# One more product in two levels, second PSUM banks begun from copies, and three vector jobs moved to ScalarE, in an attention-then-FFN kernel

## The chip, the cores and the metric

The kernel runs on one core of a Trainium2 chip. The metric is the device time of one execution in microseconds (us). Before the change it is 670.1 us, the median of three runs (669.46, 670.10, 670.87). All data are 32-bit floats in the kernel.

## The reference

```python
# batch 4, heads 8, seq 768, head_dim 64; block 64; d_ff 2048
def _attn_ref(q, k, v, lam):
    for b in range(nb):
        intra = einsum('bhic,bhjc->bhij', qb, kb) * Dmask      # lam^(i-j) for i >= j
        intra = einsum('bhij,bhjd->bhid', intra, vb)
        inter = einsum('bhid,bhde->bhie', qb * lam_pow, kv_state)
        out[:, :, sl] = intra + inter
        kb_dec = kb * rev_pow                                   # lam^(block-1-pos)
        kv_state = lam_block * kv_state + einsum('bhsd,bhse->bhde', kb_dec, vb)

def _moe_ref(x, w_in, w_out):          # x: 3072 tokens x 512
    h = x @ w_in                       # 512 x 2048, "the first product"
    g = h - np.tanh(h)
    return g @ w_out                   # 2048 x 512, "the second product"
```

The output of the attention, as 3072 rows of 512, is `x`.

## The kernel before, in words

**Tiling.** The sequence is cut into six groups g = 0 to 5 of 128 positions (of all 4 batch rows: 512 tokens). For a group the attention makes `xt` (512 features by 512 tokens), the first product with tanh makes the hidden values `g11`, `g12`, `g21`, `g22` (a two by two block matrix, each 128 partitions x 4 slices u x 512), and the second product makes four output quarters. Attention runs two groups ahead of the second product.

**Seven products in place of eight.** From group 1 on both big products use the Strassen-Winograd scheme: P1 to P7 with sums of operand blocks (`S1` to `S4` of the weights, `T1` to `T4` of the tokens), and outputs C11 = P1+P2, C12, C21 and C22 from running sums. P1+P6 is needed in three of the four outputs. Some of the seven are made by the same scheme once more ("two levels", `TWICE` for the second product, `INNER` for the first): seven steps of 128x128 blocks in place of four quarters of 128x256.

**First product of group g+1** (g+1 from 2 on; `inner_steps`, L556 to L581, and `seeded`, L485 to L520). P1, P5, P2 and P4 are in two levels. One call of `inner_steps` takes seven steps; a step is four matmuls (one per slice u), so eight records of 128x128 in the trace. The steps fill three PSUM banks (`BANKS`: y, w, z); ScalarE copies a finished corner to SBUF (L573, L575), VectorE adds the others (L577, L580). Then `seeded` handles slice by slice what is left in one level: a bank y is begun from a copy of P1 (L501), P6 is accumulated on it by four matmuls of 128x256 (L509, weights S2 in `ws[u][:, 1]`), z = y + P5 is begun by VectorE (L513); P7 goes to y, P3 to z; tanh on ScalarE and a subtraction on VectorE finish each quarter (L492, L493).

**The loop** (L949 to L1047). For g >= 2 the body is: (a) the slices u = 0 to 3: `seeded` with P7, P3 and P6 mixed with a quarter each of the second product's P1 (`down(g, 1)`); (b) `down(g, 2)`; (c) attention of group g+1 for batch rows 0 and 1 (`att_out`, `att_state`: the state update needs k times a decay, L350, and the state times a factor, L368); (d) the second product's P4, P5, P6, P7 in two levels (`down_twice`), with the scores and the attention of batch rows 2 and 3 between; (e) **the tail**: P3 of the second product turn about with P1 of the first product of group g+1 (`in_turn`), then P5 and P2, then P4 mixed with P6 and one P3 of the slices. In the tail early pieces of the attention of group g+2 (transposes, scores) are run too. g = 1 has its own body (all in one level) and makes the two-level weights: `inner_weights` (four small VectorE sums per slice, then a DMA to `fine_in` in DRAM), `factors_twice` (the same for the second product).

**Orders and queues.** Matmuls run in the written order of the program. A scheduler places VectorE's and ScalarE's instructions among each other; each engine then takes its own list in order. Weight pieces come back from DRAM over POOL's queue through a ring of eight tiles (`piece`). Inputs of the attention come over SP's queue, in written order (`load`, L146): for group g >= 3 seven sets of 16 small transposing loads of q and k (`load_blocks`, L143), then k and v in natural order for batch rows 0 and 1 (`load_natural`, L131), one more set of 16, then k and v for rows 2 and 3. `k_nat` has three buffers for four batch rows, so row 3 waits for row 0's state matmuls.

**Names.** k(g,b) below is the natural-order k of group g, batch row b (tile `k_nat`); `att_decay` multiplies it in place. A step (n,x) is step x of product Pn.

Of the kernel before, what the change touches and what calls it, by code (L numbers as in the profile page):

```python
# [15 lines left out]
AF = mybir.ActivationFunctionType  # L16
# [8 lines left out]
def kernel(  # L25
# [162 lines left out]

    INNER = (1, 5, 2, 4)
    fine_in = dram.tile([len(INNER), 3, 128, NU, 128], F32, name="fine_in")  # L190
# [156 lines left out]

    def att_decay(g, b):
        kp = raw[g, b]["k"].rearrange("s (p j) d -> s p j d", j=2)
        tied(g != 1, nc.vector.tensor_tensor(kp, kp, bwd, op=AL.mult))  # L350

    def att_state(g, bs):
        if g == NG - 1:
            return

        kv = bank("kv", "att", 4).rearrange("d (b p e) -> d b p e", b=2, p=NP)
        for n, b in enumerate(bs):
            kd, vn = raw[g, b]["k"], raw[g, b]["v"]
            if g > 0:
                att_decay(g, b)  # L360
            for p in range(NP):
                for j in range(2):
                    tied(g == 0, nc.tensor.matmul(out=kv[ts(j, 64), n, p, :], lhsT=kd[:, 2 * p + j, :],
                                                  rhs=vn[:, 2 * p + j, :], start=n == 0 and p == 0, stop=True,
                                                  skip_group_check=True))
        st = state[:, bs[0]:bs[0] + 2]
        if g > 0:
            nc.vector.tensor_tensor(st, st, lam_blk, op=AL.mult)  # L368
            nc.vector.tensor_tensor(st, st, kv, op=AL.add)
        else:  # L370
            tied(True, nc.scalar.activation(st, kv, AF.Copy))
# [109 lines left out]
    toks = {}  # L481
    LAND = {1: 12, 5: 22, 2: 11, 4: 21}
    BANKS = {1: ("yb", "z", "att"), 5: ("ya", "att", "z"), 2: ("yb", "w", "att"), 4: ("att", "att", "att")}

    def seeded(g, u, n):  # L485

        def dst(c):
            return hidden(g, c)[:, u]

        def finish(c, src):  # L490
            th = work.tile([128, 2, HB], F32, name="th", tag="th")
            nc.scalar.activation(th, src, AF.Tanh)  # L492
            nc.vector.tensor_tensor(dst(c), src, th, op=AL.subtract)  # L493

        if n == 11:
            nc.vector.tensor_tensor(dst(11), dst(11), dst(12), op=AL.add)
            finish(11, dst(11))
            return
        if n == 6:
            banks[g, u, "y"] = bank("y", "yb" if u % 2 else "ya", 1).rearrange("q (m c) -> q m c", m=2)  # L500
            nc.scalar.activation(banks[g, u, "y"], dst(12), AF.Copy)  # L501
        y = banks[g, u, "y"]
        t = banks[g, u, "z"] if n == 3 else y
        a, bname = FACT[n]
        wt = {"S3": w1[u][:, 0:2, 1], "S2": ws[u][:, 1], "S4": ws[u][:, 2]}[a]
        x = xt[g][bname]
        for m in range(2):
            for kt in range(2):
                nc.tensor.matmul(out=t[:, m, :], lhsT=wt[:, kt, ts(m, 128)], rhs=x[:, kt, :], start=False,  # L509
                                 stop=kt == 1, skip_group_check=True)  # L510
        if n == 6:
            z = banks[g, u, "z"] = bank("zs", "w" if u % 2 else "z", 1).rearrange("q (m c) -> q m c", m=2)
            nc.vector.tensor_tensor(z, y, dst(22), op=AL.add)  # L513
        elif n == 3:
            finish(12, t)
        else:
            for c in (22, 21) if u + 1 < NU else (21, 22):
                nc.vector.tensor_tensor(dst(c), dst(c), y, op=AL.add)  # L518
            for c in (22, 21) if u + 1 < NU else (21, 22):
                finish(c, dst(c))  # L520
# [6 lines left out]
    def a_quarter(n, u, i, k):  # L527
        wt = {1: w1[u][:, 0:2, 0], 2: w1[u][:, 2:4, 0], 4: w1[u][:, 2:4, 1], 5: ws[u][:, 0]}[n]
        return wt[:, k, ts(i, 128)]

    def inner_weights(u, ns):
        for n in ns:
            a11, a12, a21, a22 = (a_quarter(n, u, i, k) for i in range(2) for k in range(2))
            if n in (1, 5):
                t = hidden(GI, 22)[:, u].rearrange("p m (x c) -> p (m x) c", x=2)
            else:
                t = late["pool"].tile([128, 4, 128], F32, name="ws2", tag="sums", bufs=4)
# [15 lines left out]

    STEPS = (1, 2, 6, 5, 7, 3, 4)

    def inner_steps(g, n):  # L556

        y, w, z = (bank(x, tag, 4 if tag == "att" else 1) for x, tag in zip(("y3", "w3", "z3"), BANKS[n]))
        r5 = otile("r5")
        out4 = hidden(g, LAND[n])  # L560
        c11, c12, c21, c22 = (out4[:, :, i, ts(j, 128)] for i in range(2) for j in range(2))
        for x in STEPS:
            b = toks[g, n][x]
            wb = piece(g, ("in", n), x) if x in (3, 5, 6) else None
            dst = w if x == 2 else z if x in (3, 5) else y
            for u in range(NU):
                a = wb.rearrange("p m c -> p (m c)")[:, ts(u, 128)] if wb is not None else a_quarter(
                    n, u, *{1: (0, 0), 2: (0, 1), 7: (1, 0), 4: (1, 1)}[x])
                nc.tensor.matmul(out=dst[:, ts(u, 128)], lhsT=a, rhs=b, start=x in (1, 2, 5) and u == 0, stop=True,  # L569
                                 skip_group_check=True)  # L570
            d = dst.rearrange("q (u c) -> q u c", u=NU)
            if x in (1, 4, 6):
                nc.scalar.activation({1: c11, 4: c21, 6: c12}[x], d, AF.Copy)  # L573
            elif x == 5:
                nc.scalar.activation(r5, dst, AF.Copy)  # L575
            elif x == 7:
                nc.vector.tensor_tensor(c22, r5.rearrange("q (u c) -> q u c", u=NU), d, op=AL.add)  # L577
            else:
                c = c11 if x == 2 else c12
                nc.vector.tensor_tensor(c, c, d, op=AL.add)  # L580
            yield  # L581

# [6 lines left out]
    def in_turn(g):  # L591

        if twice(g, 3):
            turn = [a for x in STEPS for a in (("down", x), (1, x))]
        else:
            turn = [("down", 0), (1, 1), (1, 2), ("down", 1), (1, 6), (1, 5), ("down", 2), (1, 7), (1, 3), ("down", 3),
                    (1, 4)]
        return turn + [(n, x) for x in STEPS for n in (5, 2)]

    def pieces_of(g):  # L600
        if g >= GI:
            yield from ((g, ("in", 4), x) for x in (6, 5, 3))
        for n in (1, 2, 4, 5, 6, 7):
# [79 lines left out]
    def down(g, n):  # L683

        if n in (1, 2) and g >= GI:
            t, first = (bank("plain", "att", 4) if n == 1 else bank("plain", "z", 1)).rearrange(
                "q (m c) -> q m c", m=2), True
        elif n in (1, 2):
# [30 lines left out]
        else:  # L719
            o11 = late["pool"].tile([128, 512], F32, name="o11", tag="o11", bufs=1)  # L720
            nc.vector.tensor_tensor(o11, res[g, 1], t, op=AL.add)
            store(g, 11, o11)
# [226 lines left out]
    for g in range(1, NG):  # L949
        last = g == NG - 1  # L950
        (p0, p1), step = ahead, 0
        for u in range(NU):
# [16 lines left out]
            if u == 0:  # L969
                first = down(g, 1)  # L970
            for n in (1, 7) if u == 0 else (6, 3, 1, 7) if u + 1 < NU else (7, 3, 1):
                if n == 1:
                    next(first)
                else:
                    seeded(g, u + (n == 6), n)
                if n == (7 if u + 1 < NU else 3):
                    seeded_sums(g, u)
        if twice(g, 4):
# [5 lines left out]
        every(down_twice(g, 4, zw[0]) if twice(g, 4) else down(g, 4))  # L984
        run(p1[0:1])
        if g < GI:
            for u in (0, 1):
# [14 lines left out]
        run(p1[2:])  # L1002
        if g < GI:
            for u in (0, 1):
                inner_weights(u, (5,))
# [4 lines left out]
        if g < GI:  # L1010
            for u in (2, 3):
                inner_weights(u, (5,))
            every(factors_twice(2))
            load_quarters(3)
        ahead = attention(g + 2) if g + 2 < NG else ([], [])
# [4 lines left out]
        for i, (kind, x) in enumerate(in_turn(g)):  # L1020
            if kind == 2 and x == 1:
                inner_tokens(g + 1, (2,))
                if g < GI:
                    every(factors_twice(3))
                    load_quarters(4)
            if kind not in parts:
                parts[kind] = inner_steps(g + 1, kind)
            next(parts[kind])
            if (kind, x) in ((1, 7), (2, 2), (2, 7)):
                run(early_pieces[:1])  # L1030
                early_pieces = early_pieces[1:]
        for p in parts.values():
            every(p)
        inner_tokens(g + 1, (4,))
        if g < GI:
            every(factors_twice(4))
        p4 = inner_steps(g + 1, 4)
        for n in (None, None, 6, None, None, 16, None, None, 3, None):
            if n is None:
                next(p4)  # L1040
            else:
                if n == 3:
                    run(early_pieces)
                seeded(g + 1, n // 10, n % 10)
                seeded(g + 1, (6, 16, 3).index(n), 11)
        seeded(g + 1, 3, 11)
        every(p4)  # L1047

# [29 lines left out]
```

## Time and profile before

| what | value |
|---|---|
| median of the runs | 670.1 us |
| the profiled execution | 665.92 us; its span, first to last instruction, 664.2 us |
| granted TensorE clock | 1.000 |
| busy: TensorE matmuls, weight loads, VectorE, ScalarE, POOL | 98, 90, 74, 33, 35 % |
| TensorE's idle time in all | 10.0 us of waits; the longest single one 3.3 us |
| L569 (steps of the first product) | 896 matmul records of 128x128 |
| L509 (slices in one level) | 384 matmul records of 128x256 |
| L350 (decay of k) | 20 x 684 ns on VectorE |
| L368 (state's scaling) | 8 x 678 ns on VectorE |
| DMA on SP's queue | 133,536 packets, 31.5 MB, 24 % of the 16 engines |

Each trace row names line, engine, operation, tiles, shapes and count; a logical fp32 matmul has two records. "Idle before" and the arrow name what the engine waited for. TensorE's records overlap (each begins before the last has drained), so the time of a block of work is read from the starts of successive rows, not from the durations.

### The profile page before, as it was taken

What the parts mean: (1) busy time and instruction counts of PE and PEld (TensorE: products, weight loads), DVE (VectorE), ACT (ScalarE), POOL (GpSimd) and SP (SyncE); (2) the same over time, 40 slices, a digit from 0 to 9 for tenths busy, and PEclk for the clock granted to TensorE, in tenths of its full rate; (3) what the DMA queues carried; (4) which work ended last, traced back from release to release, by engine and by line L of the source; (5) the groups of instructions that cost most, each with busy time, mean ns of one, the idle gap of its engine ahead of it and who ended that gap; (6) DMA issues with size and microseconds to landing.
All of it is one profiled execution on the core that took longest, in us unless ns stands there. A gap on an engine that the chain in (4) does not pass through costs nothing.

```text
span 664.2 us, 13689 instructions
## 1 busy us (share of the span) xinstructions
PE 650.9 (98%) x5112; PEld 597.3 (90%) x5112; DVE 490.4 (74%) x923; ACT 218.7 (33%) x418; POOL 229.2 (35%) x397
## 2 busy tenths in 40 slices
PE   8899999999999999899999999999999999999998
PEld 7788888888888999798999998899998899998897
DVE  4577896745787887588997577988577988457953
ACT  3796835503221112343112243212333212333210
POOL 0001435735432557520345310255320244420261
PEclk9999999999999999999999999999999999999999
DMA  9989888969765999984698773498874376741394
GB/s 212 228 221 258 267 304 233 338 166 252 194 160 136 246 270 298 277 260 94 193 282 251 211 163 93 120 278 241 233 176 98 85 246 205 228 127 48 88 301 153
DMA packets 165475, 136.74 MB, mean 206 GB/s; under 512 B 134688, under 2 KB 135840, under 8 KB 165408
## 3 DMA queue, kind: packets, MB, share of 16 engines
q0 software_dynamic: 31728, 104.36, 49.0%
q1 hardware_dynamic: 133536, 31.50, 24.0%
q8 instruction: 41, 0.67, 0.4%
q14 instruction: 26, 0.21, 0.1%
q10 hardware_dynamic: 144, 0.00, 0.0%
HBM read 109.84 MB, written 25.95 MB: 204 GB/s over the span
## 4 chain that ended last, share of the span: by engine, by line
PE 73%; DMA 14%; SPq 7%; DVE 2%; ACT 2%; issue 1%; POOL 1%; POOLq 0%; ACTq 0%; DVEq 0%
PE y L750 10%; PE y L509 8%; PE plain L697 8%; PE zw L750 8%; PE y L569 7%; SPq L143 5%; PE h L805 5%; DMA q_blk<-in_q_dram 5%; PE zs L509 4%; PE z L569 3%; DMA k_blk<-in_k_dram 3%; PE sp L341 3%; PE op L395 3%; DMA raw<-in_moe_w_in_dram 2%; PE acc L834 2%; PE w L569 2%
## 5 line engine op out<-in xcount | busy, mean ns | idle before, releaser
L659 POOL DMA_DIRECT2D wb<-fine x147 | 79.2, 539 | 187.4 <-PE plain L697 118.0
L697 PE MATMUL plain<-wb,g 128*128 128x256 f32 x352 | 81.2, 380 | 0.0
L697 PEld LDWEIGHTS plain<-wb,g 128*128 128x128 f32 x352 | 66.1, 190 | 8.8
L753 ACT ACTIVATE q<-y 128x128 f32<-128x128 f32 x84 | 23.3, 278 | 128.9 <-PE y L750 128.1
L805 PE MATMUL h<-xt,w 128*128 128x256 f32 x256 | 57.9, 382 | 2.9 <-DVE w L285 2.9
L805 PEld LDWEIGHTS h<-xt,w 128*128 128x128 f32 x256 | 47.7, 190 | 10.5 <-DVE w L285 2.9
L750 PE MATMUL y<-wb,g 128*128 128x128 f32 x384 | 51.1, 278 | 0.0
L573 ACT ACTIVATE g<-y 128x512 f32<-128x512 f32 x48 | 28.5, 594 | 63.8 <-PE y L569 63.8
L492 ACT ACTIVATE th<-g 128x512 f32<-128x512 f32 x48 | 29.5, 628 | 59.1 <-DVE g L518 57.2
L750 PEld LDWEIGHTS y<-wb,g 128*128 128x128 f32 x384 | 46.4, 192 | 1.1 <-issue 0.3
L662 POOL DMA_DIRECT2D wb<-factors x56 | 30.3, 541 | 48.0 <-PE z L569 21.4
L206 POOL DMA_DIRECT2D raw<-in_moe_w_out_dram x16 | 8.7, 546 | 84.7 <-ACT r L282 58.1
L656 POOL DMA_DIRECT2D wb<-fine_in x48 | 25.9, 542 | 33.2 <-PE y L569 13.5
L345 DVE TENSOR_TENSOR ss<-sp,mask 128x512 f32<-128x512 f32 x48 | 30.6, 683 | 7.7 <-PE sp L341 7.7
L750 PE MATMUL zw<-wb,g 128*128 128x128 f32 x256 | 33.8, 275 | 0.0
L493 DVE TENSOR_TENSOR g<-g,th 128x512 f32<-128x512 f32 x48 | 31.7, 686 | 2.8 <-ACT th L492 2.8
L834 PE MATMUL acc<-wt,g 128*128 128x256 f32 x144 | 32.7, 380 | 0.0
L518 DVE TENSOR_TENSOR g<-g,y 128x512 f32<-128x512 f32 x32 | 20.9, 683 | 14.1 <-PE y L509 14.1
L750 PEld LDWEIGHTS zw<-wb,g 128*128 128x128 f32 x256 | 31.2, 192 | 0.0
L834 PEld LDWEIGHTS acc<-wt,g 128*128 128x128 f32 x144 | 27.3, 190 | 3.7
L509 PE MATMUL zs<-xt,ws 128*128 128x256 f32 x128 | 30.6, 381 | 0.0
L509 PE MATMUL y<-tt,ws 128*128 128x256 f32 x128 | 30.3, 379 | 0.0
(219 smaller groups left out, 1484.7 us busy)
## 6 DMA issues: line engine op xcount, KB each, us to landing
wb<-fine POOLq DMA_DIRECT2D x147, 256.0 KB, 3.9
wb<-factors POOLq DMA_DIRECT2D x56, 256.0 KB, 4.4
wb<-fine_in POOLq DMA_DIRECT2D x48, 256.0 KB, 4.5
raw<-in_moe_w_out_dram POOLq DMA_DIRECT2D x16, 512.0 KB, 5.4
v_nat<-in_v_dram SPq DMA_DIRECT2D x24, 256.0 KB, 5.5
k_nat<-in_k_dram SPq DMA_DIRECT2D x20, 256.0 KB, 4.9
fine<-wt POOLq DMA_DIRECT2D x17, 256.0 KB, 4.5
raw<-in_moe_w_in_dram SPq DMA_DIRECT2D x8, 512.0 KB, 6.0
```

The lines of the kernel that those rows point to most:

```text
L143: nc.sync.dma_start(out=x[ts(c, 32), p], in_=blk.rearrange("(r t) a -> t r a", t=32)))
L345: tied(g == 0, nc.vector.tensor_tensor(ss[:, j], sp[j], mask[:, j], op=AL.mult))
L492: nc.scalar.activation(th, src, AF.Tanh)
L493: nc.vector.tensor_tensor(dst(c), src, th, op=AL.subtract)
L509: nc.tensor.matmul(out=t[:, m, :], lhsT=wt[:, kt, ts(m, 128)], rhs=x[:, kt, :], start=False, stop=kt == 1, skip_group_check=True)
L569: nc.tensor.matmul(out=dst[:, ts(u, 128)], lhsT=a, rhs=b, start=x in (1, 2, 5) and u == 0, stop=True, skip_group_check=True)
L659: nc.gpsimd.dma_start(out=t.rearrange("p m c -> p (m c)"), in_=fine[TWICE.index(n_), SUB.index(x_)].rearrange("p u c -> p (u c)"))
L662: nc.gpsimd.dma_start(out=t, in_=factors[XAT[FACT[n_][1]]][:, 2 * x_:2 * x_ + 2, :])
L697: nc.tensor.matmul(out=t[:, m, :], lhsT=a[:, u, kt, ts(m, 128)], rhs=wb[:, kt, :], start=first and u == 0 and m == 0 and kt == 0, stop=u = ...
L750: nc.tensor.matmul(out=dst, lhsT=a[:, u, :], rhs=wb[:, ts(u, 128)], start=x in (1, 2) and u == 0, stop=u == NU - 1, skip_group_check=True)
L805: tied(u == 0, nc.tensor.matmul(out=hm[c][:, m, :], lhsT=w1[u][:, i, a, ts(m, 128)], rhs=xt[0, t][:, i, :], start=m == 0 and i == 0, stop= ...
L834: nc.tensor.matmul(out=acc[n][:, r, :], lhsT=a[:, ts(r, 128)], rhs=b, start=kt == 0 and r == 0, stop=kt == KH - 1, skip_group_check=True)
```

## The change

- **P6 of the first product in two levels.** It gets an entry in `INNER`, its own weights (`inner_weights(u, (6,))`, in the tail of g = 1, staged in the tile of `g21`), token sums and fine pieces, and steps in the tail, turn about with P4. Its results are added to P1 in the tile `g12` itself. The matmuls of `seeded` with n = 6 go; y is begun by a copy of the sum and z by one VectorE addition of two SBUF tiles.
- **Second banks begun from copies.** In `inner_steps` for n other than 1, ScalarE copies step 1's bank into the bank w, and step 2 accumulates there, so that C11 comes out of w in one instruction. For P2 and P6 VectorE's drains add `g12` (P1) at once, so that P1+P2 needs no addition later (the addition at L496 goes).
- **Steps in another order** (`INSTEPS`: 1, 5, 2, 6, 7, 3, 4), other banks, and the slices' order is P7, quarter of `down(g, 1)`, P3.
- **To ScalarE**: the decay of k for groups over 2 (eight activations of 128x64 per batch row with a scale taken from `mask`), the state's scaling for groups over 2 (four of 128x128 per half), and C11 of the second product: P2's bank is begun from a copy of P1's, and C11 is a copy.
- **Moved in g = 1**: `factors_twice(2)` to `(4)` with their loads.

```diff
-    INNER = (1, 5, 2, 4)
+    INNER = (1, 5, 2, 4, 6)
...
     def att_decay(g, b):
+        if g > GI:
+            for h in range(H):
+                k_h = raw[g, b]["k"][:, h, :]
+                nc.scalar.activation(k_h, k_h, AF.Copy, scale=mask[:, h % 2, h // 2, BLK - 1:BLK])
+            return
         kp = raw[g, b]["k"].rearrange("s (p j) d -> s p j d", j=2)
...
-            if g > 0:
+            if 0 < g <= GI:
                 att_decay(g, b)
...
-            nc.vector.tensor_tensor(st, st, lam_blk, op=AL.mult)
+            if g > GI:
+                for p in range(NP):
+                    nc.scalar.activation(st[:, :, p], st[:, :, p], AF.Copy, scale=fwd[:, p, BLK - 1:BLK])
+            else:
+                nc.vector.tensor_tensor(st, st, lam_blk, op=AL.mult)
...
-    LAND = {1: 12, 5: 22, 2: 11, 4: 21}
-    BANKS = {1: ("yb", "z", "att"), 5: ("ya", "att", "z"), 2: ("yb", "w", "att"), 4: ("att", "att", "att")}
+    LAND = {1: 12, 5: 22, 2: 11, 4: 21, 6: 12}
+    BANKS = {1: ("yb", "z", "att"), 5: ("ya", "z", "w"), 2: ("att", "yb", "att"), 4: ("att", "w", "att"),
+             6: ("att", "yb", "att")}
...
         if n == 11:
-            nc.vector.tensor_tensor(dst(11), dst(11), dst(12), op=AL.add)
             finish(11, dst(11))
             return
         if n == 6:
-            banks[g, u, "y"] = bank("y", "yb" if u % 2 else "ya", 1).rearrange("q (m c) -> q m c", m=2)
-            nc.scalar.activation(banks[g, u, "y"], dst(12), AF.Copy)
...
+            nc.scalar.activation(y, dst(12), AF.Copy)
+            nc.vector.tensor_tensor(z, dst(12), dst(22), op=AL.add)
+            return
...
+    INSTEPS = (1, 5, 2, 6, 7, 3, 4)
...
+        more = n in (2, 6)
+        filled = n != 1
+
+        def take(dst, add, src):
+            if more:
+                nc.vector.tensor_tensor(dst, add, src, op=AL.add)
+            else:
+                nc.scalar.activation(dst, src, AF.Copy)
...
+            if x == 1:
+                nc.scalar.activation(w if filled else c11, y if filled else d, AF.Copy)
+            elif x == 2:
+                if filled:
+                    take(c11, s11, d)
+                else:
+                    nc.vector.tensor_tensor(c11, c11, d, op=AL.add)
+            elif x == 6:
+                take(c12, s12, d)
             elif x == 5:
-                nc.scalar.activation(r5, dst, AF.Copy)
+                take(r, s22, d)
...
+        return turn + [(n, x) for x in INSTEPS for n in (5, 2)] + [
+            (4, 1), (4, 5), (4, 2), (6, 1), (4, 6), (6, 5), (4, 7), (6, 2), (4, 3), (6, 6), (4, 4), (6, 7), (6, 3),
+            (6, 4)]
...
-                "q (m c) -> q m c", m=2), True
+                "q (m c) -> q m c", m=2), n == 1
+            if n == 1:
+                low[g] = t
+            else:
+                nc.scalar.activation(t, low.pop(g), AF.Copy)
...
-            nc.vector.tensor_tensor(o11, res[g, 1], t, op=AL.add)
+            if g >= GI:
+                nc.scalar.activation(o11, t, AF.Copy)
+            else:
+                nc.vector.tensor_tensor(o11, res[g, 1], t, op=AL.add)
...
-            for n in (1, 7) if u == 0 else (6, 3, 1, 7) if u + 1 < NU else (7, 3, 1):
+            for n in (7, 1, 3) if u == 0 else (7, 3, 1) if u + 1 < NU else (7, 3):
...
+            if u == 1 and GI <= g < NG - 2:
+                for b in (0, 1):
+                    att_decay(g + 1, b)
...
         run(p1[0:1])
+        if GI <= g < NG - 2:
+            for b in (2, 3):
+                att_decay(g + 1, b)
...
+            if (kind, x) in ((4, 2), (4, 6), (4, 7), (4, 3)):
+                seeded(g + 1, (2, 6, 7, 3).index(x), 11)
```

The scheduler's placement in the changed program: the eight activations for k(g+1,0) and those for k(g+1,1), written at u = 1 of the slices of group g, stand on ScalarE already in the tail before, among the drains of P4: after step (4,1)'s copy and two tanh comes the first of k(g+1,0); behind it, in this order, two more tanh, the drains of (4,5), (4,2), the copy of (6,1) and the drain of (4,6), mixed with the rest of k(g+1,0); then k(g+1,1), the last drain of P4, the two copies into y, and k(g+1,2). k(g+1,3) stands between the copies of the second product's P4. SP's list of transfers is the same as before.

## The prediction

> **What bounds the kernel now.** First I read the page's busy times, then who waited for whom.
>
> ```profile
> PE 650.9 (98%) x5112; PEld 597.3 (90%) x5112; DVE 490.4 (74%) x923; ACT 218.7 (33%) x418; POOL 229.2 (35%) x397
> PE y L569 <- DVE g L577: 3.3, 1, 3.3
> ```
>
> TensorE is the bound: it idles 10 us in all, and only one wait after the first 100 us is long, 3.3 us. So matmuls taken away count in full, and so does each us in which TensorE stands. What a block costs is read from starts in TensorE's timeline (tail of g = 2):
>
> ```profile
> 382.36 1.95 PE L569 MATMUL y<-tt,w 128*128 128x128 f32 x16
> 384.15 1.06 PE L569 MATMUL w<-tt,w 128*128 128x128 f32 x8
> 385.04 1.89 PE L509 MATMUL y<-tt,ws 128*128 128x256 f32 x8
> 386.77 1.05 PE L569 MATMUL y<-tt,wb 128*128 128x128 f32 x8
> ```
>
> A step of eight 128x128 records takes 0.89 us, eight records of 128x256 take 1.73. The first row holds step (2,4) and then (4,1), which so starts at 383.25. Next, how that one wait came about (VectorE's timeline, then TensorE's):
>
> ```profile
> 271.62 0.69 DVE L577 TENSOR_TENSOR g<-r,y 128x512 f32<-128x512 f32 x1 [3.15 <-PE y L569]
> 277.05 0.69 DVE L645 TENSOR_TENSOR gS<-gS 128x512 f32<-128x512 f32 x1 [4.75 <-DMA gS<-factors]
> 277.66 0.68 DVE L577 TENSOR_TENSOR g<-r,y 128x512 f32<-128x512 f32 x1
> ...
> 278.40 2.05 PE L569 MATMUL y<-tt,w 128*128 128x128 f32 x16 [3.31 <-DVE g L577]
> ```
>
> L577's bank was full long before, but L645 stood ahead of it on VectorE and waited 4.75 us for a transfer; so L577 was late, and TensorE after it. An engine's list is not left out of order here: a wait for a transfer stops what stands behind it. [...]
>
> Last, the queue that brings k (SP's timeline):
>
> ```profile
> 278.65 14.58 SPq L143 DMA_DIRECT2D q_blk<-in_q_dram  x16
> 293.34 0.42 SPq L131 DMA_DIRECT2D k_nat<-in_k_dram  x1
> 293.81 0.58 SPq L131 DMA_DIRECT2D v_nat<-in_v_dram  x1
> 294.50 0.80 SPq L131 DMA_DIRECT2D k_nat<-in_k_dram  x1
> ...
> 381.01 8.48 SPq L143 DMA_DIRECT2D q_blk<-in_q_dram  x16
> 389.58 0.38 SPq L131 DMA_DIRECT2D k_nat<-in_k_dram  x1
> ...
> 390.70 2.51 SPq L131 DMA_DIRECT2D k_nat<-in_k_dram  x1
> ```
>
> k(3,0) is issued at 293.34 (3.4 us to landing: there at 296.7) and k(4,0) at 389.58 (5.0: 394.6), because seven sets of 16 small loads stand before them. VectorE asked for k(3,0) only at 320.65 (L350), so this lateness was free.
>
> **Part by part.**
>
> *P6 in two levels.* Taken away per group: four slices of eight 128x256 records, 4 x 1.73 = 6.91 us. Added: seven steps, 7 x 0.89 = 6.25. Saved 0.66 for each of four groups: -2.6 us.
>
> *Drains.* Per group the inner steps go from 12 to 19 large VectorE additions (3, 2, 2, 6, 6 for P1, P5, P4, P2, P6); L496's four and C11's one go; four small token sums come. That is 2 large ones at 0.60 us (spacing of L681's rows) and 4 of 0.29 more, 2.4 us, and 3.6 less in groups 3 and 4, where decay and scaling leave. The tail of g = 2 has room: VectorE is busy 9.6 of 16 us from 368 to 384 and 8.3 of 12 from 384 to 396. In the slices TensorE has 3 x 1.73 = 5.18 us per slice now (P6 is gone from 6.91), VectorE nine operations, 5.43. The lag, 4 x 0.25, is covered by `down(g, 2)` (6.9 us) and the attention (3.9), since sums are needed only by the next product. Priced at nothing; without cover 1 us per group. The copies into second banks (0.6 us each on ScalarE) have two or more steps, 1.8 us, before their bank is used, and P1's copy for C11 the 3.5 us of the last slice.
>
> *Weights in g = 1.* 16 sums of 0.28 us, four writes of 192 KB, three more pieces of 256 KB per group. They lie ahead of the first wait below, which swallows up to 16 us of lateness.
>
> *State's scaling.* Eight activations of 128x128 (278 ns, L753's row) per group after `att_out`'s reads; they end before the second copy of `down_twice` is due. Nothing.
>
> *Decay on ScalarE, first place: the tail of g = 1.* The eight activations of k(3,0) stand among P4's drains. No row has a 128x64 activation. From 594 ns at 512 and 278 at 128 elements it is 225 ns; bounds 140 (two copies in a row overlap by 90, L399) and 278. [...]
>
> Without the old 3.3 us wait, (2,4) starts at 275.1 and (4,1) at 276.0. TensorE then does (4,1), the scores (1.1 us), (4,5), (4,2), (6,1), (4,6), (6,5), and at 282.5 needs the drain of (4,6), which must be out of y before (4,7). On ScalarE that drain stands behind k(3,0). When does k(3,0) land? As before at 296.7; but once TensorE stops, POOL's ring of eight stops too, so the last set of 16, which took 14.6 us beside POOL's transfers, goes faster (the fastest set in SP's timeline takes 7.6: landing 290), while the new weight traffic delays it (300, if 1.6 MB at some 290 GB/s are half in its way). At 282.5 four of the 16 are out at the old pace; twelve at 7.6 / 16 take 5.7, and 0.4 and 3.4 more give 292. With 2 us for the new traffic I take 294. From landing to the end of that drain ScalarE has six activations of k and six of 128x512 (0.6 each): 1.35 + 3.6 = 4.95 us. So TensorE goes on at 298.95, having stood 16.4 us. Then eight steps (7.1) and sixteen blocks of 1.73 (seven, three and both quarters of `down`: 27.6) lead to `att_out` at 333.7; before, it began at 321.56 (L389). **+12.2 us**, the lost 3.3 us wait and this group's 0.66 in it; bounds +8 and +18.
>
> What is late next: k(3,1), 3.1 us behind, finds ScalarE 5 us behind; k(3,2), 12.2 behind, is asked for 14 behind. Both covered, by 1.8 us at the least.
>
> *Second place: the tail of g = 2.* SP starts group 4's sets after k(3,3), issued at 325.07 when row 0's state matmuls are done; I count from there. k(4,0) lands at +69.5. TensorE reaches (4,1) at 383.25 - 325.07 = +58.2, and (4,7) after 1.1 + 6 x 0.89 at +64.7. It goes on at 69.5 + 4.95 = +74.5 (9.7 us), and gets to `att_out` at +109.2 against 425.43 - 325.07 = 100.4. **+8.8 us.** The pace is steady: group 4's seven sets took 62.9 us, group 5's 64.1; with landings from 3.1 to 7.3 us the bounds are +6 and +12.
>
> *k(3,3) and k(4,3)* are asked for after the second copy of `down_twice`'s P4, 3.1 us into it. k(4,3) landed at 432.0, 2.7 us in; the next copy is due at 5.4 us, and seven activations end at 4.7. Nothing.
>
> *Tails of g = 3 and 4* have no decay (the condition on g): -0.66 each, -1.3.
>
> **Sum.** 12.2 + 8.8 - 1.3 = +19.7 us. On the profiled execution, 665.9 (span 664.2), that is 685.6; the median of the runs is 4.2 above that execution, so 670.1 + 19.7 = **689.8 us**.
>
> **Rivals.**
>
> *No wait binds* (ScalarE gets k in time, the change does what it is for): 670.1 - 2.6 - 3.3 = 664.2. For it: ScalarE is busy 33% only. Against: k(3,0) would have to land 16 us earlier, with SP issuing without a gap from 215 to 293. Chance 0.04.
>
> *Only the first binds*, if group 4's sets run at the fastest pace, 7 x 7.6 = 53 us, and k(4,0) lands 9.6 us earlier: the second place gives -0.9 in place of 8.8, so 680.1. For it: POOL's traffic shifts; against: 62.9 and 64.1 in two groups. Chance 0.12.
>
> *VectorE becomes the bound of the slices*: the uncovered lag of 1 us in each of four groups on top of the forecast, 694. For it: 5.43 against 5.18; against: the cover above. Chance 0.10.
>
> *The first wait is longer*: the new weight writes hold SP's set back further than 300, or k(3,2) takes more than 1.8 us longer and ScalarE waits a second time, before the first tanh of the slices: +6 or more, about 697. For it: the DMA engines are 92 to 97% busy from 236 to 292. Chance 0.16.
>
> *Forecast*: both places as worked out. Chance 0.58, its own range 683 to 697.
>
> **How the numbers follow.** The low end is the second rival's, 680; the high end takes both upper bounds, 670.1 + 18 + 12 - 1.3 = 699. Left out is the first rival and the far end of the last, under 2 in 10. A measurement of this kernel tells 0.2%, 1.3 us, from no change; faster by more only with the first rival, 0.04; within it only if both waits nearly vanish, 0.01; slower 0.95.
>
> **What would show it.** In the tails of g = 1 and g = 2 of the changed kernel: ScalarE idle before a 128x64 activation of `k_nat`, released by its DMA, some 14 and 8 us long; right after it TensorE idle at a step of the first product, released by ScalarE's drain, near 16 and 10 us; none in the tails of g = 3 and 4. L509 with 256 records in place of 384. Wrong would be: those waits absent, a VectorE release in the slices, or a wait at k(3,2), k(3,3).

## The result, and the profile after

The changed kernel takes 702.4 us (median of six runs, 699.6 to 705.9); the kernel before, run beside it, 669.7. The ratio is 1.0495, 95% interval 1.0453 to 1.0537. The forecast was 689.8 with a range up to 699: the sign and the two waits were right, the size was 12.6 us short. A time is the median of all runs, but a ratio leaves out an execution over 1.5% above the fastest of its kernel, and there are two: 687.3 us with the decay back on VectorE, and 712.7 with the quarters back and the decay on ScalarE.

First the two waits, in the view of who waited for whom (us in total, count, longest):

```profile
ACT k_nat L352 <- DMA k_nat<-in_k_dram: 26.7, 4, 14.8
...
PE y L589 <- ACT g L580: 21.6, 2, 10.8
...
PE z L589 <- DMA wb<-fine_in: 4.9, 4, 2.0
```

ScalarE waits for k in four places, of which two are long (14.81 and 10.35 us), and TensorE twice behind these, as forecast. The last line was not forecast: TensorE also waits for weight pieces of the first product. Now the first place, ScalarE's timeline:

```profile
301.36 0.59 ACT L352 ACTIVATE k_nat<-k_nat,mask 128x64 f32<-128x64 f32 x2 [14.81 <-DMA k_nat<-in_k_dram]
301.86 0.61 ACT L502 ACTIVATE th<-g 128x512 f32<-128x512 f32 x1
...
305.32 0.58 ACT L580 ACTIVATE g<-y 128x512 f32<-128x512 f32 x1
305.80 2.48 ACT L352 ACTIVATE k_nat<-k_nat,mask 128x64 f32<-128x64 f32 x10
```

and TensorE's in the same microseconds:

```profile
291.71 1.16 PE L589 MATMUL y<-tt,wb 128*128 128x128 f32 x8 [2.42 <-DMA wb<-fine_in]
293.51 1.71 PE L589 MATMUL z<-tt,wb 128*128 128x128 f32 x8 [0.64 <-DMA wb<-fine_in]
305.95 2.07 PE L589 MATMUL y<-tt,w 128*128 128x128 f32 x8 [10.74 <-ACT g L580]
307.82 1.91 PE L589 MATMUL w<-tt,ws 128*128 128x128 f32 x8
309.52 1.74 PE L589 MATMUL z<-tt,wb 128*128 128x128 f32 x8
311.10 1.06 PE L589 MATMUL y<-tt,wb 128*128 128x128 f32 x8
```

The drain of (4,6) at 305.32 stands behind k(3,0), and releases step (4,7) at 305.95. The first three steps behind the stand then take 311.10 - 305.95 = 5.15 us in place of 3 x 0.89 = 2.68. The windows (length; busy time of TensorE's matmuls, its weight loads, VectorE, ScalarE, POOL; granted clock; share of the DMA engines; GB/s) tell why:

```profile
294.00:305.90 11.90, 1.21 (x6) 0.92 (x5) 2.26 (x4) 4.54 (x13) 2.59 (x5) 0.50 0.99 273
305.90:311.10 5.20, 5.15 (x25) 5.15 (x25) 2.30 (x4) 2.38 (x10) 0.54 (x1) 0.51 0.66 146
311.10:318.00 6.90, 6.90 (x52) 6.48 (x51) 4.65 (x7) 1.72 (x3) 1.63 (x3) 1.00 0.81 175
```

While TensorE stands here the granted clock is 0.50, and it is 0.51 in the first 5.2 us of work. (It had gone down a little sooner: it is 1.00 from 291.7 to 293.8 and 0.50 from 293.9 to 295.2, behind two shorter waits for pieces and ahead of the stand.) The second place has it too, with a mean clock of 0.67 in the stand and 0.69 in the 5.2 us behind it (TensorE's timeline: 4.29 us from the first start to the last, for 2.68 us of steps):

```profile
423.81 2.08 PE L589 MATMUL y<-tt,w 128*128 128x128 f32 x8 [10.85 <-ACT g L580]
425.68 1.69 PE L589 MATMUL w<-tt,ws 128*128 128x128 f32 x8
427.21 1.06 PE L589 MATMUL z<-tt,wb 128*128 128x128 f32 x8
428.10 1.06 PE L589 MATMUL y<-tt,wb 128*128 128x128 f32 x8
```

Read from the starts of `att_out`'s first matmuls (L389 before, L398 after), the stages of the two profiled executions compare so, in us. The groups are those of the attention; expectations below that name a stage go by the loop's g, one less, so that their stage from group 1's last `att_out` to group 2's first is the first place here.

| stage | before | after | difference | forecast |
|---|---|---|---|---|
| start to group 2's second `att_out` | 237.31 | 240.19 | +2.9 | 0 |
| to group 3's first (first place) | 84.25 | 103.40 | +19.2 | +12.2 |
| to group 3's second | 25.12 | 25.16 | 0 | 0 |
| to group 4's first (second place) | 78.75 | 91.84 | +13.1 | +8.8 |
| to group 4's second | 25.10 | 26.16 | +1.1 | 0 |
| to group 5's first | 78.74 | 78.89 | +0.2 | -0.7 |
| to group 5's second | 24.22 | 24.23 | 0 | 0 |
| to the end | 110.7 | 111.7 | +1.0 | -0.7 |

The sum is +37.4 against +32.6 between the medians. The profiled execution of before is one of its fastest: its clock was 1.000. Of the 51 runs of the kernel before that stood beside the experiments, the five with a mean clock of 1.000 average 666.3 us, the 23 with 0.997 668.5, the 19 with 0.995 or 0.994 670.6 and the four with 0.992 672.9. So the kernel before usually loses some clock as well.

### The profile page after: what moved, and what is told of

Same layout as the page of the kernel before. It is cut to its first block, busy times and chain, and to the rows that moved or that the text cites. A ratio compares the mean times of both kernels' runs of the same rounds, so it can differ in the third digit from the quotient of the medians.

```text
span 701.6 us, 14027 instructions
## 1 busy us (share of the span) xinstructions
PE 657.6 (94%) x5208; PEld 603.9 (86%) x5208; DVE 496.0 (71%) x951; ACT 243.2 (35%) x506; POOL 239.0 (34%) x413
## 4 chain that ended last, share of the span: by engine, by line
PE 67%; DMA 14%; SPq 7%; ACT 3%; POOL 3%; issue 3%; DVE 2%; POOLq 0%; ACTq 0%; DVEq 0%
PE y L785 10%; PE plain L729 9%; PE y L589 7%; PE zw L785 7%; PE h L840 5%; SPq L143 4%; PE zs L521 4%; PE y L521 4%; PE z L589 4%; PE op L404 2%; DMA k_nat<-in_k_dram 2%; PE sp L341 2%; DMA raw<-in_moe_w_in_dram 2%; PE acc L869 2%; PE w L589 2%
## 5 line engine op out<-in xcount | busy, mean ns | idle before, releaser
L684 POOL DMA_DIRECT2D wb<-fine_in x60 | 32.5, 543 | 43.6 <-PE y L589 15.2
L589 PE MATMUL y<-tt,w 128*128 128x128 f32 x160 | 22.6, 292 | 21.6 <-ACT g L580 21.6
L589 PEld LDWEIGHTS y<-tt,w 128*128 128x128 f32 x160 | 20.8, 205 | 22.1 <-ACT g L580 22.1
L589 PE MATMUL z<-tt,wb 128*128 128x128 f32 x256 | 35.0, 283 | 2.9 <-DMA wb<-fine_in 2.9
L580 ACT ACTIVATE g<-y 128x512 f32<-128x512 f32 x24 | 14.3, 596 | 61.4 <-PE y L589 61.4
L589 PEld LDWEIGHTS z<-tt,wb 128*128 128x128 f32 x256 | 32.1, 198 | 3.6 <-DVE g L550 2.0
```

The costliest lines, as they stand in the source:

```text
L684: nc.gpsimd.dma_start(out=t.rearrange("p m c -> p (m c)"), in_=fine_in[INNER.index(n_[1]), (5, 6, 3).index(x_)].rearrange("p u c -> p (u c)"))
```

## The experiments

In each group of runs the kernel before was run on the same chip; the ratios are to it, with 95% intervals.

### The decay alone

The decay back on VectorE (one part undone):

```diff
     def att_decay(g, b):
-        if g > GI:
-            ...
-            return
...
-            if 0 < g <= GI:
+            if g > 0:
                 att_decay(g, b)
```

> The changed kernel with one part undone: the decay of k is back on VectorE, in att_state, for every group. Theory (k's lateness binds only because the decay stands among the drains on ScalarE; the low clock follows from TensorE's stand): both stands of 10.8 us and the two stretches of low clock go, att_out of the second group comes about 84 us after the one before it, as before the change (84.25), not 103.4; time 662 to 671. Rival (the two-level P6 itself, its 19 large additions and its weights, costs the time): the stages stay above 95 us and the time at 690 or more. Something between, 675 to 685, would mean that the waits for weight pieces in the tail of g = 1 bind by themselves.

678.5 us, ratio 1.0115 (1.006 to 1.017). Both stands are gone, and by the ratios 25.5 of the 33.2 us with them; the second place takes 78.72 us. But 1.15%, 7.7 us, remain, the "something between" of the expectation: the first place takes 90.16 us, not 84. TensorE's timeline there:

```profile
264.26 1.51 PE L584 MATMUL z<-xt,wb 128*128 128x128 f32 x8 [1.81 <-DMA wb<-fine_in]
265.57 3.26 PE L724 MATMUL plain<-wb,g 128*128 128x256 f32 x8
...
287.41 1.13 PE L584 MATMUL z<-tt,wb 128*128 128x128 f32 x8 [1.52 <-DVE ss L345]
...
292.15 1.16 PE L584 MATMUL y<-tt,wb 128*128 128x128 f32 x8 [1.83 <-DMA wb<-fine_in]
294.42 1.13 PE L584 MATMUL z<-tt,wb 128*128 128x128 f32 x8 [1.10 <-DMA wb<-fine_in]
```

Four waits make 6.3 us, and the eight records of L724 take 268.67 - 265.57 = 3.1 us in place of 1.73: behind a wait of 1.81 us the clock was low, 0.72 from 264 to 270 us.

That is not all that remains. This profiled execution is 14.0 us longer than that of the kernel before: 3.1 before group 2's second `att_out`, 5.9 in the first place, 0.8 at the end, and 4.3 in the stage to group 5's first `att_out` (83.03 us for 78.74). In that stage a drain of the first product waits on ScalarE for an output write, and TensorE behind it (ScalarE's timeline, then TensorE's):

```profile
478.81 0.60 ACT L575 ACTIVATE r<-z 128x512 f32<-128x512 f32 x1 [6.49 <-DMA out_dram<-q]
```

```profile
479.62 1.80 PE L780 MATMUL y<-wb,g 128*128 128x128 f32 x8 [2.58 <-ACT q L783]
```

The kernel before has no such wait for `out_dram` on ScalarE, the changed one has 8.4 us of it. No experiment undoes it alone.

The other way round, the kernel before with only the decay moved (the diff's lines for `att_decay` and its calls):

> The kernel before with one part of the change alone: the decay of k for groups 3 and 4 on ScalarE, emitted where the change emits it. Theory: the same two stands of TensorE appear in the tails of g = 1 and g = 2, and with them the low clock; +18 to +28 us, 688 to 698. Rival (the decay is harmless, the two-level P6 costs it): 668 to 673.

691.5 us, ratio 1.0323 (1.0276 to 1.037): the theory. TensorE stands 10.66 and 6.39 us. k(3,0) was there 80.5 us after the issue of k(2,3).

The decay on ScalarE, kept at its written place:

```diff
-                nc.scalar.activation(k_h, k_h, AF.Copy, scale=...)
+                tc.keep_in_program_order(nc.scalar.activation(k_h, k_h, AF.Copy, scale=...))
```

> The changed kernel with the decay still on ScalarE, but kept behind the slices' work ahead of which it was written, in the order of the program, so that k(3,0) and k(4,0) are asked for about 15 us after they land. Theory (it is the place in ScalarE's list, not ScalarE): no wait for k, no stand, 662 to 673; the 16 activations in a row, about 4 us, may delay one tanh of the slices by 1 or 2 us a group. Rival (32 activations of 0.25 us are too much work for ScalarE wherever they stand): 685 or more.

679.8 us, ratio 1.015 (1.0108 to 1.0192). No wait for k is left. It falls between the two ranges, but its interval overlaps that of the decay on VectorE: the two long waits came of the place in ScalarE's list, not of the engine. The 16 activations take 3.92 us in a row (ScalarE's timeline, 316.22), behind k's landing. They are not quite free: the 16 for rows 2 and 3 stand ahead of a copy that TensorE waits for, and the two stages from first to second `att_out` of groups 3 and 4 take 26.40 us each in this profile, for 25.12 with the decay on VectorE.

### The clock behind a stand

```diff
             if (kind, x) == (4, 7) and g in (1, 2):
+                fill = bank("fill", "ya", 1)
+                for _ in range(22):
+                    nc.tensor.matmul(out=fill, lhsT=ident, rhs=mask[:, 0]..., start=True, stop=True)
```

> The changed kernel with 22 matmuls of 128x512, whose sums nobody reads, set into TensorE's list just ahead of step (4,7) in the tails of g = 1 and g = 2, so that TensorE is busy (22 x 0.43 = 9.5 us) through most of the stand of 10.8 us. The wait for k stays as it is. Theory (the granted clock falls because TensorE stands, and the steps after it pay for it): the clock right after stays near 1.0, a step takes 0.89 us again, and the time falls by 3 to 6 us, to 696 to 699. Rival (the low clock comes from elsewhere, or costs nothing): 701 to 704. A third: the work itself delays, 705 or more.

716.1 us, ratio 1.0688 (1.062 to 1.0757): the third case. I had priced a matmul at one record; it has two (the seven of the next run are 14 in its trace), and the filling outlasted the stand (21.10 and 19.05 us). The time so says nothing on the clock, but the profile does: behind the filling the first three steps take 320.41 - 317.73 = 2.68 us in the first place and 443.14 - 440.46 = 2.68 in the second, 0.89 each.

With 7 in place of 22:

> As the run with 22 matmuls put into the stand, but with 7. In that run the 22 took 21.1 us (0.86 us each at full clock, since each of 128x512 is two passes, not one), and so outlasted the stand by 10 and 6 us. Seven take about 6 us at full clock and some 9 us where the clock is low when they begin; the stand ahead of step (4,7) is 9 to 11 us, so that they end before the drain releases TensorE. Theory (the clock falls through the stand, and the steps behind it pay some 2.5 us in each place): the steps after the release take 0.89 us, 697 to 700. Rival (nothing is paid there): 701 to 704. Outlasting the stand would show as 705 or more.

700.6, 701.0, 710.2 and 710.3 us; ratio 1.0541 (1.0479 to 1.0602). As a time this is inconclusive. The profile, of a run at 710.3, shows both what the filling does and what it moves; TensorE's timeline in the second place:

```profile
418.63 6.17 PE L1075 MATMUL fill<-mask,ident 128*128 128x512 f32 x14
425.17 1.16 PE L589 MATMUL y<-tt,w 128*128 128x128 f32 x8 [0.36 <-ACT g L580]
426.16 1.06 PE L589 MATMUL w<-tt,ws 128*128 128x128 f32 x8
427.06 1.06 PE L589 MATMUL z<-tt,wb 128*128 128x128 f32 x8
427.95 1.06 PE L589 MATMUL y<-tt,wb 128*128 128x128 f32 x8
...
439.76 3.78 PE L521 MATMUL y<-xt,w 128*128 128x256 f32 x8 [5.15 <-ACT y L511]
```

Without the stand the three steps take 2.78 us, not 4.29, at a granted clock of 1.00 (415 to 433) in place of 0.69. So the stand causes the low clock here, and it costs 1.5 us. (In the first place seven were too few: TensorE still stood 4.34 us.) Then ScalarE waits 9.23 us for k(4,2), and TensorE 5.15: the second wait that the prediction's fourth rival had put at k(3,2).

### What else the change costs

The kernel before with one more row in a scratch tensor (only `INNER = (1, 5, 2, 4, 6)`):

> The kernel before with only the list of the first product's two-level blocks made longer by the sixth, so that the scratch tensor fine_in has five rows in DRAM in place of four; the fifth is neither written nor read. In all four kernels with the longer tensor the first att_out of group 1 started at 74.2 to 75.7 us, in the two without at 72.4 and 72.7. Theory (the place of the tensors in DRAM makes the loads of the first 75 us slower): att_out at 74 to 76, 671 to 674. Rival (chance, or something else in the changed program): 72.3 to 72.8, 668 to 671.

669.6 us, ratio 1.0003 (0.9981 to 1.0025); `att_out` at 72.79. The rival holds. Its profile shows by chance what the kernel before, by its mean clocks, does in most runs; TensorE's timeline behind its one wait:

```profile
279.61 3.78 PE L569 MATMUL y<-tt,w 128*128 128x128 f32 x16 [4.05 <-DVE g L577]
283.19 1.91 PE L569 MATMUL w<-tt,w 128*128 128x128 f32 x8
284.89 2.25 PE L509 MATMUL y<-tt,ws 128*128 128x256 f32 x8
```

The first row took 2.05 us in the execution shown before (278.40), whose granted clock was 1.00 from 278.0 to 282.4; here it is 0.50 from 279.0 to 283.4. This stage takes 87.84 us here and 84.25 there: 0.7 us more of waiting, and the other 2.9 put down to the low clock (an estimate: what is left).

P6's sub-weights left out, the decay on VectorE:

```diff
-                    for u in range(NU):
-                        inner_weights(u, (6,))
...
-            elif x in (3, 5, 6):
+            elif x in (3, 5, 6) and kind != 6:
                 yield g + 1, ("in", kind), x
```

> The changed kernel with the decay back on VectorE and, beside that, without the preparation of P6's sub-weights: no sums for them in the tail of g = 1, no writes to DRAM, no pieces streamed; P6's seven steps and drains run as before on quarters that lie in SBUF, so that P6's product is not the reference's. Theory (what is left of the loss once the decay is back on VectorE is POOL's queue in the tail of g = 1, where TensorE waited 5.5 us for pieces and 1.5 for VectorE): that stage takes 80 to 84 us in place of 90.2, the time is 668 to 673. Rival (the steps and drains of P6 cost it): the stage stays at 88 or more, 676 to 681.

671.6 us, ratio 1.0031 (1.001 to 1.0052); the stage takes 87.56 us. The time is the theory's, by the ratios 5.6 us below the kernel with them; the stage is near the rival's bound, since two waits for pieces, 1.77 and 1.86 us, stay. So the mechanism is the theory's only in part: between the two profiles the first place is 2.6 us shorter, and the stage to group 5's first `att_out` 3.3, where ScalarE's wait for the output write is 4.88 in place of 6.49.

The early quarters alone, in the kernel before:

```diff
         run(p1[2:])
         if g < GI:
+            every(factors_twice(2))
+            load_quarters(3)
...
+            if g < GI and (kind, x) == (1, 7):
+                every(factors_twice(3))
+                load_quarters(4)
```

> The kernel before with one move that the change also makes: the differences and loads of the second product's quarters for P4 and P7 a few steps earlier (ahead of down_twice's P7, and after step (1,7)), nothing else. Theory (VectorE's wait of 4.75 us for a load of these quarters caused TensorE's one wait of 3.3 us): the wait goes, 665 to 668. Rival (the loads move other pieces on POOL's queue back, and TensorE waits for those): 669 or more.

675.8 us, ratio 1.0104 (1.0075 to 1.0134): the rival. POOL's timeline, then TensorE's:

```profile
264.97 2.68 POOL L656 DMA_DIRECT2D wb<-fine_in  x5 [4.72 <-DMA fine_in<-g]
267.64 2.15 POOL L646 DMA_DIRECT2D fine<-gS  x4
273.75 0.76 POOL L633 DMA_DIRECT2D gS<-factors  x1 [3.96 <-DMA fine<-gS]
275.55 1.50 POOL L633 DMA_DIRECT2D gS<-factors  x2 [1.05 <-DMA fine<-gS]
277.89 0.75 POOL L633 DMA_DIRECT2D gS<-factors  x1 [0.84 <-issue]
278.63 1.09 POOL L656 DMA_DIRECT2D wb<-fine_in  x2
```

```profile
282.50 2.05 PE L569 MATMUL z<-xt,wb 128*128 128x128 f32 x8 [6.34 <-DMA wb<-fine_in]
```

The move does away with the wait of 3.3 us and puts one of 6.34 in its place. A load of quarters here waits until the writes out of the same tile have landed (3.96 us), and the pieces stand behind it on POOL's queue: the piece of 278.63 is late for TensorE.

The quarters back, the decay on VectorE, P6 in two levels:

> The changed kernel with the decay back on VectorE, and with the differences and loads of the second product's quarters back at the steps where the kernel before has them; P6 in two levels stays, with its sums, writes and pieces. The decay alone undone gave 678.5; the early quarters alone, in the kernel before, cost 6.7 us. Theory (what remained of the loss was the early quarters, which stand on POOL's queue ahead of the pieces): 668 to 673, and the stage from group 1's last att_out to group 2's first takes 82 to 88 us. Rival (P6's own writes and pieces cost it): 676 to 680, with waits for pieces of fine_in as long as before.

674.1 us, ratio 1.0077 (1.0042 to 1.0113), still 5.2 above the kernel before; the stage takes 86.88 us, with waits for pieces of 3.05, 1.14 and 0.86. The time is above the theory's range, the stage within it. The interval overlaps that of the decay alone undone (1.006 to 1.017), so that in the changed kernel a share of the quarters is not shown.

The last differences two steps of P4 later, in the kernel before:

```diff
-        if g < GI:
-            every(factors_twice(4))
         p4 = inner_steps(g + 1, 4)
-        for n in (None, None, 6, None, None, 16, None, None, 3, None):
+        for i, n in enumerate((None, None, 6, None, None, 16, None, None, 3, None)):
+            if g < GI and i == 2:
+                every(factors_twice(4))
```

> The kernel before with one move: the last differences of quarters (those for P3) two steps of P4 later, so that on VectorE both drains of step 7 come ahead of the first difference that waits for a load. Theory (the one wait of 3.3 us in the kernel before comes of the order on VectorE, and in most runs the clock falls behind it, as in the run with the longer scratch tensor, whose wait of 4.05 us was followed by sixteen blocks in 3.8 us in place of 1.95): the wait goes and the clock stays at 1.0; 663 to 667. Rival (the load is late for TensorE by another way, or the wait goes to the slices): 668 or more.

664.2 us (663.9 to 666.2), ratio 0.9922 (0.9891 to 0.9952): 0.8% faster than the kernel before. VectorE's timeline:

```profile
272.43 0.69 DVE L577 TENSOR_TENSOR g<-r,y 128x512 f32<-128x512 f32 x1 [3.45 <-PE y L569]
273.33 0.69 DVE L577 TENSOR_TENSOR g<-r,y 128x512 f32<-128x512 f32 x1 [0.21 <-PE y L569]
...
279.52 0.68 DVE L645 TENSOR_TENSOR gS<-gS 128x512 f32<-128x512 f32 x1
```

Both drains now come ahead of the difference, which finds its load landed. TensorE's longest wait behind the first 100 us is 0.8, and the clock is 0.997 or above in all six runs.

Last, the same two causes with the decay left on ScalarE:

> The changed kernel with the decay left on ScalarE, and only the differences and loads of the quarters back at the steps where the kernel before has them. With the decay on VectorE this move alone took the time from 678.5 to 674.1. Theory A (the step of the prediction: lateness ahead of the first wait for k is swallowed by it, since the release is set by k's landing): 701 to 704, no change. Theory B (POOL's traffic also moves k's landing): k(3,0) lands nearer to 78.8 us after the issue of k(2,3), where it came 83.3 after it in the changed kernel, and the time is 696 to 700.

> The changed kernel with the decay left on ScalarE, without the sums, writes and pieces of P6's sub-weights (its steps run on quarters that lie in SBUF, so that P6's product is not the reference's). With the decay on VectorE this took the time from 678.5 to 671.6. Theory A (swallowed by the first wait): 701 to 704. Theory B (the traffic moves k's landing): 694 to 699, and k(3,0) lands 79 to 81 us after the issue of k(2,3).

698.1 us, ratio 1.041 (1.0339 to 1.048), and 699.4, ratio 1.0444 (1.0375 to 1.0514). The first time lies in theory B's range, the second between the two; but both intervals overlap that of the changed kernel, so the theories are not told apart by time. The first one's only profile is of the execution of 712.7 us, and nothing is read from it. In the second TensorE reached (4,7) sooner and stood longer, 15.66 us, and went on at 307.37, no earlier than in the changed kernel (305.95). k(3,0) was there 302.78 - 218.65 = 84.1 us after k(2,3) was issued: the landing did not come earlier without P6's traffic, and the waits for pieces that fell away ahead of it gained nothing. That is theory A, on one profile, of the longest of four executions (703.3 us; the others 693.3 to 700.4).

## Why the prediction was short, step by step

**The mechanism of the decay: right; its price right by luck.** ScalarE did not go round the waiting instruction: it stood 14.81 us at k(3,0), and the drain of (4,6), whose bank was full before 293.51, came behind it, at 305.32. The row from which the prediction took this is VectorE's; that ScalarE does the same was the author's assumption until these runs. The two stands are where they were put. Without what it had set against them (the old wait of 3.3, twice 0.66), the prediction priced the decay at 12.2 + 8.8 + 3.3 + 1.3 = 25.6 us. Undoing it gives 25.5, doing it alone costs 21.6. But the parts do not agree: the forecast has 16.2 and 9.5 us for the two places, and the stages with and without the decay differ by 103.40 - 90.16 = 13.2 and 91.84 - 78.72 = 13.1. Two errors cancel. In the first place TensorE stood 10.74 us, not 16.4: it was to reach (4,7) at 282.5 - 237.31 = 45.2 us after group 2's second `att_out` and reached it at 295.2 - 240.19 = 55.0, having waited 7.3 us for pieces on the way. In the other direction, both releases came late, and the clock was low behind them. From k's landing to the release the prediction said 4.95 us; 4.59 and 4.58 were measured.

**"k(3,0) ... I take 294": the step that failed.** Counted from k(2,3)'s issue, it was to land at 294 - 215.17 = 78.8 us and landed at 301.36 - 218.04 = 83.3. The last set of 16 and the issue behind it were sized right, by SP's timeline after:

```profile
283.37 9.52 SPq L143 DMA_DIRECT2D q_blk<-in_q_dram  x16
292.99 0.38 SPq L131 DMA_DIRECT2D k_nat<-in_k_dram  x1
...
294.12 6.30 SPq L131 DMA_DIRECT2D k_nat<-in_k_dram  x1
```

The forecast gives the set 9.6 us (3.85 at the old pace and 5.7), and it took 9.52; with the 2 us for the new traffic it has the issue at 75.0, and it came at 292.99 - 218.04 = 75.0. The pace of the set was luck, since the reason given for it, that TensorE stops, does not hold: its stand began at 295.2, behind the set, and with the decay on VectorE, where that stand is absent, the set took 10.59. What failed is the time from issue to landing: 301.36 - 292.99 = 8.4 us, with the DMA engines 0.99 busy, where the prediction had 3.8 (0.4 and 3.4, read in the kernel before). That makes 4.5 of the 7 us by which the first place exceeds the forecast. In the second place k(4,0) landed at 419.23 - 347.13 = 72.1, forecast 69.5: 2.6 us. What in the change makes k(3,0) late stays open. It landed 80.5 to 81.7 us after k(2,3)'s issue in the five profiles with the old tail (80.5 with the decay alone), and 82.5 to 87.7 in the eight read here with the new one, also without P6's weights (82.5 and 84.1) and with the quarters back (86.4).

**Missing: the clock.** No term priced what a stand does to the steps behind it, 2.5 and 1.5 us. With the late landings these make 4.5 + 2.6 + 2.5 + 1.5 = 11.1 of the 17.7 us by which the difference of the two profiles, 37.4, exceeds the 19.7 of the forecast; 2.9 of the rest lie at the start, where the cause is open. In the changed kernel the granted clock is 0.50 up to the release and 0.51 in the 5.2 us behind the stand of 10.74, 0.67 and 0.69 in the second place. The profile from which the prediction was made shows no such loss: 1.00 from 278.0 to 282.4, behind its one long wait of 3.31. Behind shorter waits the clock went either way (last section).

**"Without the old 3.3 us wait" and "Weights in g = 1": priced at nothing, and not free.** The old wait went, but in the kernel before the early quarters alone cost 6.7 us (675.8 against 669.2), while the later place of the last differences, of which the change has the like, takes the wait away at a gain of 4.7. With the decay on VectorE the weights cost 5.6 us by the ratios; what the quarters cost there is not told from nothing. All but the decay was forecast at -3.3 - 4 x 0.66 = -5.9 us and measured, with the decay undone, at +7.7. Part of that is POOL's queue, on which a load that waits (3.96 us in the run with the early quarters alone) holds up the pieces; part is ScalarE's wait for an output write, and part the start. The prediction said that lateness ahead of the first wait is swallowed by it. Nothing in the runs contradicts that for the changed kernel: without the weights, or with the quarters back, its time is not told from 702.4.

**P6 "saved 0.66" per group: nothing came of it.** The second place takes 78.72 us with P6 in two levels (decay on VectorE), 78.75 before. The matmuls are fewer as counted; but in this stage eight steps of the first product follow the one before by 0.93 to 1.01 us in place of 0.89, where the kernel before has two. Six more at some 0.07 us would be 0.4 of the 0.66 (an estimate from the rows, not tried).

**"k(3,3) and k(4,3) ... Nothing": mis-sized by 1 us.** ScalarE waits 1.27 us for k(4,3), and TensorE 0.90 for the next copy; that is the +1.1 of that stage.

**The rivals.** The nearest was the first wait being longer (697), but neither of its ways came: counted from k(2,3)'s issue its bound of 300 is 84.8, and k(3,0) landed at 83.3, as late without the weight writes that it named (84.1); and ScalarE waited for k(3,2) only 0.27 us. The others did not happen; no wait for VectorE stands in the slices.

**The base.** The sum was added to a median that itself holds low clock behind the old wait, as the run with that wait removed shows (4.7 us for a wait of 3.3).

## What to carry to other kernels

When an operation moves to an engine with time to spare, look up when its input lands and what stands behind it in that engine's list; kept later in the list, the same work cost 1.3 us in two stages and neither of the two long waits. When loads are moved on a shared queue, price what is queued behind them, above all if a load must wait for a write from the same tile (3.96 us here). And count a stand of the matrix engine as longer than it looks: here the granted clock was 0.51 in the 5.2 us behind a stand of 10.7, which cost 2.5 us more.

## What the runs showed of the hardware beyond that

Behind short waits the clock went either way. With the decay on VectorE, behind 1.81 us, eight records of 128x256 took 3.1 us in place of 1.73, at a granted clock of 0.72; behind 2.00 us in the changed kernel (264.26) the eight that came next took 1.75, and in the run with the quarters back and the decay on VectorE the clock was 1.00 (236 to 292) with a wait of 3.05 us in it. And in all profiles of kernels with the change's tail `att_out` of group 1 begins at 73.3 to 76.3 us, in those without it at 72.4 to 73.0, though the work up to there is the same; the longer scratch tensor is not the cause (72.79 with it alone), and what is stays open.
